# Attention and gated MLP on one core: paired items in one PSUM bank, output transposed in place, whole-tile key reads, and engine orders rewritten by a table

## The chip, the cores and the metric

The kernel runs on one core of one Trainium2 chip. A core has five engines that run side by side, each through its own list of instructions and in order: TensorE (PE) multiplies matrices and writes PSUM, VectorE (DVE) and ScalarE (ACT) read PSUM and compute elementwise, GpSimd (POOL) computes elementwise in SBUF, and SyncE (SP) issues DMA transfers. PEld is the weight-load half of PE, and SPq in a trace is SP's queue of DMA issues. PSUM has eight banks of 512 fp32 columns by 128 partitions. The metric is the device time in microseconds, lower is better.

## The reference

```
mod = silu(c) @ w_mod                       # six vectors of 640: sa, ca, ga, sb, cb, gb
h = layernorm(x) * (1 + ca) + sa            # x: 2048 tokens x 640
q, k, v = h @ wqkv                          # 32 heads of 20
o = softmax(q k^T / sqrt(20)) v             # every token against all 2048
x = x + ga * (o @ wo)
h = layernorm(x) * (1 + cb) + sb
x = x + gb * (((h @ w_gate) * (h @ w_up)) @ w_down)     # inner width 1536
```

All inputs are bf16. There are 32 x 2048 x 2048 exponentials, some 134 million, and they are the largest elementwise job by far.

## The kernel before

**Tiling.** Queries are cut into seven chunks (512 tokens, then six of 256) and heads into eight sets of four. A pair of chunk and set is an *item*. The four heads of a set lie in four strips of 32 partitions, so a score matmul has 32 rows of contraction (20 used) and four strips can work at once. The smallest job is a *unit*: one strip, 512 columns of scores for 128-row key tiles, one PSUM bank.

**Two ways to an exponential.** Most units go in twos to ACT: line 1524 writes two banks (0 and 1, or 3 and 4, by turns), line 1561 takes the exponential of 1024 columns into a slot of `PP`. The rest go to DVE in quads of four units: line 1585 reads a bank into `DB` as a scaled int16, lines 1617 and 1625 mask it into two bf16 factors in `DSS`, and their product is formed by POOL in four pieces (line 1637) or by DVE in one (line 1622). `QUADS` says how many quads each item gives to DVE. Line 2192 multiplies `PP` and `DSS` with the values `Vf` (a column of ones in front gives the softmax sum) and accumulates the item in one bank; column tiles of 32 work four abreast.

**End of an item.** `item_end_tasks` (line 1707): a DVE transpose `OT` (1717), a reciprocal of the sums (1723), the normalised `OTn` (1725, on POOL or DVE), a transpose back into `OcT` (1734), and 20-row DMA moves into `Ocp` (1746), since heads of 20 rows have to be packed into the 128-row blocks that w_o expects.

**Projections.** Queries, keys and values are multiplied while the first chunk is already in attention. Keys and queries that can't be written in place go as packed rows to `k_rows` and `q_rows` in DRAM (1276) and come back in strips of 32: `KT` by four transfers for a tile (1289), `QT` by one (1298). `Ocp` also serves as the source of zeros for `q_rows` (1450).

**MLP.** `suffix` (line 1773) does the output projection of a finished chunk, the second layernorm, gate and up, and down, in between the scores of the next chunk. Weights of gate and up stream through staging tiles (1931). For 256 tokens a gate round and an up round share one bank: DVE casts the gate half (1959), and multiplies it with the up half (1966).

**Order.** Nothing is written in order by hand. Each piece of work is a `Task` with an engine, an assumed duration and dependences; `Sched` plays them out in assumed time, and `emit_program` writes each engine's list in the order found, with semaphore waits for what comes from other engines. For PE, `pick_pe` chooses at each step: the next score if its banks are free, a DVE score that is due, attention times values, then projection and MLP work by priority. `STAGE` changes its thresholds item by item. When recent PE work falls under `FILL_MIN`, `zero_fill` adds matmuls of zeros into an open accumulator (2523). Banks 5, 6, 2 and 7 form the pool `G`, handed to whoever asks first: DVE's scores, accumulators of items, projections and MLP rounds:

```
G = Slots([5, 6, 2, 7], "G")
...
def avail(self, only=None):
    best = None
    for k, (i, rel) in enumerate(self.free):
        ...
        for r in rel:
            t = max(t, r.done + SEM)
        if best is None or t < best[0]:
            best = (t, k)
```

## Time and profile before

| | |
|---|---|
| runs shown | 804.77 us median of 3 (804.38 to 808.84) |
| span of the profiled execution | 803.8 us, first to last instruction |
| instructions in it | 37761 |
| exponentials on ACT (line 1561) | 810, 748.5 us busy |
| scores read by DVE (line 1585) | 428, 285.5 us busy |
| DMA | 64.66 MB, mean 80 GB/s |

The profiled execution is one of the same program; its own time is the span and what lies around it, and only the span has rows. "Idle before" is the time an engine stood still ahead of a group of instructions, with what ended it. Matmuls overlap, and their ends are modelled, so the busy share of PE isn't a measure of its load. Windows give busy time of each engine in a stretch, and PEclk the granted clock of PE as a share of full speed.

### The profile page before, as it was taken

Reading aid. Unit: us, or ns where it says so; the run is one execution under the profiler, and the core shown is the slowest. Engines: PE = TensorE matmul, PEld = TensorE weight load, DVE = VectorE, ACT = ScalarE, POOL = GpSimd, SP = SyncE. Lnnn points to the kernel's source line nnn. Section 1 sums busy time; section 2 is a strip of 40 time slices with the busy share of each in tenths; the row PEclk is TensorE's granted clock in tenths of the full one; section 3 lists DMA queues with packets and bytes.
Section 4 is the critical chain, followed back from the end, with each engine's and each line's share of the span. In section 5 each row is a group of like instructions: output and inputs, shape, how many; then the busy total and the mean of one; then the engine's idle time right before and its main releaser. Section 6 shows DMA issues by size and latency. Waiting matters only on the chain.

```text
span 803.8 us, 37761 instructions
## 1 busy us (share of the span) xinstructions
PE 790.4 (98%) x16595; PEld 380.6 (47%) x16595; DVE 697.8 (87%) x1401; ACT 764.8 (95%) x847; POOL 386.0 (48%) x396
## 2 busy tenths in 40 slices
PE   8999999999999999999999999999999999999998
PEld 4433433333244434445555455555555555555567
DVE  7978788799989999988999999999899988898754
ACT  6899899999999999999999999999999999999961
POOL 3347455654366565763444443545534554455300
PEclk9999999999999999999999999999999999999999
DMA  9733212212341532120032404231540254414420
GB/s 297 243 113 91 62 43 64 61 33 76 92 109 50 167 88 52 35 55 13 24 81 65 95 16 112 57 73 39 121 89 15 54 118 94 98 37 106 92 68 18
DMA packets 154314, 64.66 MB, mean 80 GB/s; under 512 B 116951, under 2 KB 154151, under 8 KB 154151
## 3 DMA queue, kind: packets, MB, share of 16 engines
q1 hardware_dynamic: 153223, 61.10, 30.0%
q8 instruction: 132, 2.16, 1.1%
q10 hardware_dynamic: 928, 1.15, 0.5%
q14 instruction: 31, 0.25, 0.1%
HBM read 50.63 MB, written 8.99 MB: 74 GB/s over the span
## 4 chain that ended last, share of the span: by engine, by line
PE 77%; ACT 14%; DVE 5%; issue 2%; DMA 1%; SPq 1%; POOL 0%; DVEq 0%; ACTq 0%
PE ps_all L1524 26%; PE ps_all L970 21%; PE ps_all L2192 19%; ACT PP L1561 14%; PE ps_all L1230 4%; PE ps_all L966 3%; DVE DB L1585 2%; PE ps_all L1889 1%; PE ps_all L1166 1%; PE ps_all L1127 1%; DVE DSS L1617 1%; PE ps_all L2523 0%; DVE DSS L1625 0%; DMA QT<-q_rows 0%; PE ps_all L991 0%
## 5 line engine op out<-in xcount | busy, mean ns | idle before, releaser
L1561 ACT ACTIVATE PP<-ps_all 128x1024 bf16<-128x1024 f32 x810 | 748.5, 1090 | 6.7 <-PE ps_all L1524 4.8
L1637 POOL TENSOR_TENSOR DSS<-DB,DSS 128x512 bf16<-128x512 bf16 x268 | 305.0, 1157 | 290.6 <-DVE DSS L1625 254.2
L1585 DVE TENSOR_SCALAR DB<-ps_all 128x512 int16<-128x512 f32 x428 | 285.5, 681 | 50.5 <-PE ps_all L1524 48.0
L1524 PE MATMUL ps_all<-QT,KT 32*128 32x256 bf16 (+2 forms) x3648 | 319.4, 287 | 4.5 <-DMA QT<-q_rows 0.8
L1524 PEld LDWEIGHTS ps_all<-QT,KT 32*128 32x128 bf16 x3648 | 93.9, 92 | 204.1 <-ACT PP L1561 141.5
L2192 PE MATMUL ps_all<-PP,Vf 128*32 128x256 bf16 (+2 forms) x2892 | 163.6, 291 | 0.5 <-DVE KPB L1242 0.3
L970 PE MATMUL ps_all<-h2T,stg 128*32 128x256 bf16 (+2 forms) x2716 | 122.9, 281 | 0.3 <-DVE DB L1585 0.2
L2192 PEld LDWEIGHTS ps_all<-PP,Vf 128*32 128x32 bf16 (+1 forms) x2892 | 54.5, 94 | 76.4 <-issue 67.6
L2192 PE MATMUL ps_all<-DSS,Vf 128*32 128x256 bf16 (+1 forms) x1512 | 88.7, 291 | 0.0
L1617 DVE TENSOR_SCALAR DSS<-DB 128x2048 int16<-128x2048 int16 x107 | 77.2, 722 | 0.8
L970 PEld LDWEIGHTS ps_all<-h2T,stg 128*32 128x32 bf16 x2716 | 61.6, 96 | 26.9 <-issue 22.0
L1625 DVE TENSOR_SCALAR DSS<-DB 128x2048 int16<-128x2048 int16 x107 | 73.2, 684 | 0.8 <-PE ps_all L2192 0.8
L970 PE MATMUL ps_all<-wd,hprod 128*32 128x320 bf16 (+1 forms) x1404 | 61.0, 277 | 0.0
L1725 POOL TENSOR_TENSOR OTn<-OT,invT 128x256 bf16<-128x256 f32 (+1 forms) x49 | 35.3, 721 | 37.7 <-DVE invT L1723 37.5
L1622 DVE TENSOR_TENSOR DSS<-DB,DSS 128x2048 bf16<-128x2048 bf16 x40 | 51.5, 1287 | 0.0
L2192 PEld LDWEIGHTS ps_all<-DSS,Vf 128*32 128x32 bf16 x1512 | 36.5, 95 | 20.9 <-issue 12.4
L970 PE MATMUL ps_all<-wV,hT 128*32 128x160 bf16 x1280 | 38.9, 236 | 0.9 <-DVE DB L1585 0.3
L970 PEld LDWEIGHTS ps_all<-wd,hprod 128*32 128x32 bf16 x1404 | 31.2, 96 | 14.2 <-issue 10.8
L1717 DVE STREAM_TRANSPOSE OT<-ps_all 128x256 f32<-128x256 f32 (+2 forms) x57 | 27.1, 475 | 8.8 <-PE ps_all L2192 8.5
L1230 PE MATMUL ps_all<-hT,wk 128*32 128x512 bf16 x360 | 32.3, 382 | 0.0
L970 PEld LDWEIGHTS ps_all<-wV,hT 128*32 128x32 bf16 x1280 | 24.6, 97 | 15.9 <-issue 8.2
L1230 PE MATMUL ps_all<-hT,wq 128*32 128x512 bf16 x375 | 31.3, 382 | 0.6 <-DVE OT L1717 0.6
(133 smaller groups left out, 556.1 us busy)
## 6 DMA issues: line engine op xcount, KB each, us to landing
stg<-in_B_w_gate_dram SPq DMA_DIRECT2D x74, 160.0 KB
stg<-in_B_w_up_dram SPq DMA_DIRECT2D x74, 160.0 KB
KT<-k_rows SPq DMA_DIRECT2D x112, 32.0 KB
QT<-q_rows SPq DMA_DIRECT2D x48, 64.0 KB
Ocp<-OcT SPq DMA_DIRECT2D x164, 10.0 KB
wm<-in_w_mod_dram SPq DMA_DIRECT2D x3, 800.0 KB
x<-in_A_x_dram SPq DMA_DIRECT2D x7, 320.0 KB
k_rows<-KPA SPq DMA_DIRECT2D x16, 128.0 KB
```

Of the source, the lines that this page charges most:

```text
L970: return lambda e, b: e.matmul(ps[32 * x:32 * x + 32, b, c0 + o:c0 + o + w], lhs()[:, 32 * x:32 * x + 32], rhs() if w == n else rhs()[:, o ...
L1230: f = [lambda e, b_, k=k, x=x: e.matmul(ps[x:x + min(32, w - x), b_, :], wx[:, k, r0 + x:r0 + min(x + 32, w)], hT[tc][:, k, :], tile_posit ...
L1524: ems.append(lambda e, i=i, kt=kt: e.matmul(dstf()[:, i * u.n:(i + 1) * u.n], KT[32 * u.s:32 * u.s + 32, u.j, kt * 128:(kt + 1) * 128], QT ...
L1561: return e.activation(PPs[g % 2][:, cellp["p"], 0:nu * 512], ps[:, b0:b0 + nu, :].rearrange("p b c -> p (b c)"), AFT.Exp, scale=ESCALE)
L1585: return e.tensor_scalar(DBl[st_["slot"]][:, x * 512:(x + 1) * 512], bank(cell["b"]), EBIAS, 0.0, op0=ALU.add, op1=ALU.max)
L1617: return e.tensor_scalar(DSl[st_["ss"][0]][:, :], DBl[st_["slot"]][:, :], 0x7F, 0x3F00, op0=ALU.bitwise_and, op1=ALU.bitwise_or)
L1622: return e.tensor_tensor(d, DBl[st_["slot"]][:, :].bitcast(BF16), d, ALU.mult)
L1625: return e.tensor_scalar(DSl[st_["ss"][1]][:, :], DBl[st_["slot"]][:, :], 0x7F80, 2, op0=ALU.bitwise_and, op1=ALU.bitwise_or)
L1637: return e.tensor_tensor(d, DBl[st_["slot"]][:, x * w:x * w + w].bitcast(BF16), d, ALU.mult)
L1717: t1 = Task("dve", n * 1.1 + 70, lambda e: e.transpose(OT[:, 0:n], ps[:, item_info[it]["bank"], 0:n].rearrange("p (b q r) -> p b r q", q=3 ...
L1725: f3 = lambda e: e.tensor_tensor(OTn[:, 0:n].rearrange("p (b c r) -> p b r c", c=32, r=2), OT[:, 0:n].rearrange("p (b r c) -> p b r c", c= ...
L2192: ems.append(lambda e, i=i, kt=kt, stt=stt, stp=stp: e.matmul(ps[32 * s:32 * s + mc, bk, 0:u.n], Vf[:, (kt * H + 4 * u.j + s) * VW:(kt * H ...
```

## The change

1. `own`, `lead`, `second`: two neighbouring items of 256 tokens share one accumulator bank, the second in columns 256 to 511. One transpose of 512, one reciprocal and two normalisations close both.
2. `OTn` is laid out so that a transpose writes `Ocp` directly; `OcT` and its DMA moves are gone. Rows of `Ocp` come in another order, so w_o is loaded in 48 pieces in that order, and its own late extra tile is gone.
3. `join_reads`: the four transfers of a key tile become one of 128 rows, at the place of the first.
4. For 256 tokens two gate rounds share a bank, and two up rounds (`GU2`): casts and products of 512 columns.
5. `Ring` and `visit`: `PP` is 16 slots of 512; a score takes the next units from a look-ahead of six, in different strips; its two output slots needn't be neighbours.
6. `QUADS`, `STAGE` and other constants change. DVE gets 109 quads in place of 107.
7. The planner's latencies get corrections by pair of engines (`seen_at`).
8. After planning, `replan` drops 14 tasks of PE, hands out the banks of `G` from a written string for what starts after 80 us of planned time, moves tasks within each engine's list by a table, and `rechain` renews the dependences on banks.

In the listing of the changed program PE has 16538 instructions (16597 before), DVE 1278 (1403), POOL 420 (400), SP 420 (709).

```
-QUADS = ((0, 4, 3, 3, 3, 4, 4, 4), (2, 2, 1, 2, 2, 2, 1, 2), (2, 2, 1, 2, 2, 2, 1, 2), (2, 2, 1, 2, 2, 2, 1, 2), (2, 2, 1, 2, 2, 2, 1, 2), (2, 2, 1, 2, 2, 2, 1, 2), (2, 1, 2, 2, 2, 1, 2, 0))
+QUADS = ((0, 5, 3, 3, 3, 4, 3, 4), (2, 2, 2, 2, 2, 2, 1, 2), (1, 2, 1, 2, 2, 2, 1, 2), (1, 3, 1, 1, 2, 2, 1, 3), (2, 2, 1, 2, 3, 1, 1, 2), (2, 2, 1, 2, 2, 1, 2, 3), (2, 1, 2, 1, 1, 2, 4, 3))
...
+PLAN_FROM = 80000.0
+PLAN = {
+    "drop": (1947, 1963, 2320, 2729, 3476, 3487, 3498, 4099, 4112, 4723, 5191, 5496, 5497, 5901),
+    "banks": (
+        "7527657577656576575677576565765672625256225562655256657627552275227752772557225722757266252652665265"
...
+    "pe": [
+        (129, 128), (153, 144), (134, 146), (135, 147), (136, 148), (137, 149), (155, 164), (166, 186), (167, 187), (168, 188),
...
+def join_reads(sc):
+    first = {}
+    for t in sc.order["sp"]:
+        if t.whole and id(t) not in first:
+            parts, f = t.whole
+            for x in parts:
+                first[id(x)] = t
+            t.emits = [f]
...
+def rebank(sc):
+    k = 0
+    for r in sc.G.recs:
+        r["move"] = r["task"] is not None and r["task"].start >= PLAN_FROM
+        if r["move"]:
+            r["i"] = int(PLAN["banks"][k])
+            r["put"](r["i"])
+            k += 1
...
+def replan(sc):
+    gone = set(PLAN.get("drop", ()))
+    sc.order["pe"] = [t for i, t in enumerate(sc.order["pe"]) if i not in gone]
+    rebank(sc)
+    for eng, moves in PLAN.items():
...
+        old = sc.order[eng]
+        gone = {a for a, _ in moves}
+        new = [t for i, t in enumerate(old) if i not in gone]
+        for a, b in moves:
+            new.insert(b, old[a])
+        sc.order[eng] = new
+    rechain(sc)
...
+                    for t in kt_ready[(j, tc)]:
+                        t.whole = (kt_ready[(j, tc)], lambda e, j=j, tc=tc: e.dma_start(
+                            KT[:, j, tc * 512:(tc + 1) * 512],
+                            bass.AP(KS.tensor, (656 * tc + 80 * j) * 512, [[DH * 512, 4], [512, 32], [1, 512]])))
...
-    d_wo = [dma("sp", 128 * KD * D * 2, lambda e: e.dma_start(wo_sb[:, :, :], wov[:, :, :]), [d_wm[3][0]], prio=10)]
+    d_wo = [[] for _ in range(KD)]
+    for j in range(NSET):
+        i0 = DH * j
+        while i0 < DH * j + DH:
+            i1 = min(DH * j + DH, i0 // 32 * 32 + 32)
+            for x in range(4):
...
+                    return e.dma_start(wo_sb[p0:p0 + i1 - i0, i0 // 32, :], A_wo[r0:r0 + i1 - i0, :])
...
+                o = PP[:, p[0]:p[-1] + 1:(p[1] - p[0] if nu > 1 else 1), :]
+                return e.activation(o, ps[:, b0:b0 + nu, :], AFT.Exp, scale=ESCALE)
...
+                OTn[:, g0:g0 + gn, DH * (j + x):DH * (j + x) + DH, :].rearrange("p b c r -> p b r c"),
...
+            def f4(e):
+                o = Ocp[slot][:, b0:b1, qo:qo + nq_].bitcast(F32).rearrange("p k (b c) -> p k b c", c=32)
+                i = OTn[:, g0:g0 + gn, 32 * b0:32 * b1, :].rearrange("p b (k c) r -> p k b (c r)", c=32).bitcast(F32)
...
+                return e.transpose(o, i)
...
+            if n <= 256 and GU2:
+                two.append((wbuf, dm))
...
+                for w_ in range(2):
+                    mms = []
+                    for x in range(2):
+                        for k in range(KD):
+                            f = qf(n, lambda k=k, cell=pair[x][0][w_]: cell["t"][:, k, :], lambda k=k: h2T[:, k, 0:n],
+                                   k == 0, k == KD - 1, x * n)
...
-            stt = first_pv[(it, s)]
+            stt = first_pv[(it, s)] and it not in lead
...
-                ps[32 * s:32 * s + mc, bk, 0:u.n],
+                ps[32 * s:32 * s + mc, binfo["bank"], c0:c0 + u.n],
...
+    join_reads(sc)
+    replan(sc)
     nw = emit_program(nc, sc)
```

1011 lines of the change are left out of this document (679 added, 332 removed), and 289 rows, old and new, of the table PLAN.

## The prediction

> **What bounds the kernel now.** I read the page's table of engines first, then its chain, and distrusted both: TensorE (PE) is busy 98% of the span and holds 77% of the chain, ScalarE (ACT) 95% and 14%. Which of the two sets the pace is not in those shares. It is in the starts of the exponentials.
>
> ```profile
> span 803.8 us, 37761 instructions
> PE 790.4 (98%) x16595; PEld 380.6 (47%) x16595; DVE 697.8 (87%) x1401; ACT 764.8 (95%) x847; POOL 386.0 (48%) x396
> PE 77%; ACT 14%; DVE 5%; issue 2%; DMA 1%; SPq 1%; POOL 0%; DVEq 0%; ACTq 0%
> ...
> L1561 ACT ACTIVATE PP<-ps_all x810: 1002/1067/1327, 16.4 to 774.7; 128x1024 bf16<-128x1024 f32 x162
> ```
>
> The last row is the view of line 1561: 810 exponentials, the first starting at 16.4 us and the last at 774.7. The same view, cut to windows, gives the next four rows (exponentials in the window, first and last start). The waits between 100 and 775 us give the fifth.
>
> ```profile
> L1561 ACT ACTIVATE PP<-ps_all x21: 1017/1130/1255, 408.6 to 426.7; 128x1024 bf16<-128x1024 f32 x21
> ...
> L1561 ACT ACTIVATE PP<-ps_all x81: 1002/1042/1230, 16.4 to 99.5; 128x1024 bf16<-128x1024 f32 x81
> ...
> L1561 ACT ACTIVATE PP<-ps_all x11: 1017/1024/1062, 87.0 to 99.5; 128x1024 bf16<-128x1024 f32 x11
> ...
> L1561 ACT ACTIVATE PP<-ps_all x138: 1017/1125/1327, 649.1 to 774.7; 128x1024 bf16<-128x1024 f32 x138
> ...
> PEld ps_all L1524 <- ACT PP L1561: 125.4, 439, 0.8
> ```
>
> Where ACT is never short of scores, 20 steps take 18.1 us: a pace of 0.905 us for each exponential. In the last row the weight load of a score waited 439 times for an exponential to free its banks, in a stage of some 730: more often than not PE is there first. So ACT's pace is the floor, and what lies above it is lateness. The span is four terms: first start 16.4; 809 steps of 0.905 = 732.1; lateness 774.7 - 16.4 - 732.1 = 26.2; and 803.8 - 774.7 = 29.1 from the last exponential's start to the end. The lateness splits: up to 99.5 us 83.1 - 80 x 0.905 = 10.7, of which 12.5 - 10 x 0.905 = 3.4 in the stretch from 87.0 on; after 99.5 us 675.2 - 729 x 0.905 = 15.5. The last 125.6 us lose only 125.6 - 137 x 0.905 = 1.6.
>
> **The change part by part.** Counts of the changed program come from its listing of instructions by engine.
>
> Exponentials: 806 in place of 810, since DVE takes 109 quads of scores instead of 107. Four steps, -3.6 us. For 464 of them the two output slots of the new ring don't lie side by side. No row shows an exponential with such an output; a gain is excluded because the element count is the same, and the nearest bound above is the step itself: at +0.01 us each, 4.6 us. I take 0, since both halves are still 512 contiguous elements.
>
> SP's queue. The timeline from 87 to 95 us shows what the stretch at 87.0 lost: four small moves of attention output stood ahead of two reads of query tiles, and a score waited for the second until 94.31. The next rows are the durations of the issues.
>
> ```profile
> 87.61 2.98 SPq L1746 DMA_DIRECT2D Ocp<-OcT  x4
> ...
> 90.71 0.92 SPq L1298 DMA_DIRECT2D QT<-q_rows  x2
> ...
> 94.31 0.40 PE L1524 MATMUL ps_all<-QT,KT 32*128 32x512 bf16 x4 [0.82 <-DMA QT<-q_rows]
> ...
> L1746 SPq DMA_DIRECT2D Ocp<-OcT x248: 549/714/1642, 59.6 to 769.2; - x124
> ...
> L1289 SPq DMA_DIRECT2D KT<-k_rows x112: 302/421/1722, 30.1 to 195.9; - x112
> ...
> L1493 SPq DMA_DIRECT2D wo<-in_A_wo_dram x4: 327/396/1384, 33.1 to 36.2; - x4
> ```
>
> All 248 output moves go (248 x 0.714 = 177 us of issue), because a transpose now writes Ocp directly. The key reads fall from 112 to 28 (84 x 0.421 = 35 us less); w_o rises from 5 issues to 48 (43 x 0.396 = 17 us more). In the new listing these two reads follow the writes of their rows at once, with nothing between, so they go out at least the 3.0 us earlier that the four moves took: of the 3.4 us lost, 3.0 come back. The key read still waits for the same writes of k_rows, but now four strips wait for 128 KB together; behind it on SP stand w_o pieces and further key reads. Its cover is the lead at which the rows are written. With the cover gone a tile would be as late as the query read above: 94.31 - 90.71 = 3.6 us, for 28 tiles at most 101 us, and earliness gains at most the three issues saved ahead of the last strip. I take 0: the view of line 1289 names no engine that waited for a key read, though the last strip's piece always went out three issues after the first. The w_o pieces are scaled before the first use at 228.8 us:
>
> ```profile
> L970 PE MATMUL ps_all<-wo,Ocp x656: 232/299/311, 228.8 to 699.7; 128*32 128x320 bf16 x116, 128*32 128x160 bf16 x48
> ```
>
> In the listing they are issued between the key reads, the last of which starts at 195.9 us in the kernel before. That is tens of microseconds of cover; without it the output projection, and the score behind it on PE, would wait.
>
> VectorE (DVE). These rows group its instructions by shape (count, busy us, mean ns).
>
> ```profile
> L1585 DVE TENSOR_SCALAR DB<-ps_all 128x512 int16<-128x512 f32 x428 | 285.5, 681 | 50.5 <-PE ps_all L1524 48.0
> L1617 DVE TENSOR_SCALAR DSS<-DB 128x2048 int16<-128x2048 int16 x107 | 77.2, 722 | 0.8
> L1625 DVE TENSOR_SCALAR DSS<-DB 128x2048 int16<-128x2048 int16 x107 | 73.2, 684 | 0.8 <-PE ps_all L2192 0.8
> L1622 DVE TENSOR_TENSOR DSS<-DB,DSS 128x2048 bf16<-128x2048 bf16 x40 | 51.5, 1287 | 0.0
> L1959 DVE CAST gsb<-ps_all 128x256 bf16<-128x256 f32 x60 | 24.6, 412 | 4.7 <-PE ps_all L970 4.6
> L1717 DVE STREAM_TRANSPOSE OT<-ps_all 128x256 f32<-128x256 f32 x47 | 20.8, 442 | 4.8 <-PE ps_all L2192 4.7
> L1966 DVE TENSOR_TENSOR hprod<-ps_all,gsb 128x256 bf16<-128x256 f32 x48 | 19.7, 413 | 0.5
> L1734 DVE STREAM_TRANSPOSE OcT<-OTn 128x128 f32<-128x128 f32 x47 | 14.2, 301 | 1.5 <-POOL OTn L1725 1.5
> L1723 DVE RECIPROCAL invT<-OT 128x8 f32<-128x8 f32 x47 | 8.9, 189 | 0.2
> L1997 DVE TENSOR_TENSOR hprod<-ps_all,gsb 128x512 bf16<-128x512 f32 x12 | 8.1, 677 | 0.4 <-PE ps_all L970 0.4
> L1986 DVE CAST gsb<-ps_all 128x512 bf16<-128x512 f32 x12 | 8.1, 674 | 0.5 <-PE ps_all L970 0.5
> L1717 DVE STREAM_TRANSPOSE OT<-ps_all 128x512 f32<-128x512 f32 x8 | 5.7, 712 | 1.4 <-PE ps_all L2192 1.3
> L1725 DVE TENSOR_TENSOR OTn<-OT,invT 128x256 bf16<-128x256 f32 x5 | 3.1, 620 | 0.0
> ```
>
> Paired items: 46 transposes of 256 go, 23 of 512 come: -20.3 + 16.4 = -3.9; 23 reciprocals fewer: -4.3; 28 transposes of 128 fewer (two of double size more, about 0.9): -7.5. Gate and up in pairs: 60 casts and 60 products of 256 become 30 and 30 of 512: -4.5 and -4.5. Two quads more: eight score reads, two of each mask: +5.4 + 2.8. Five products of 2048 fewer: -6.4. Five more normalisations on DVE, at no more than the 0.62 us of a full one: +3.1. In all about -20 us of 697.8. DVE is not the floor, so none of it counts directly; what it buys is PSUM banks that come free sooner.
>
> GpSimd (POOL): 296 pieces of the product instead of 268, 28 x 1.157 = +32 us, covered by 290 us of its own idle time; if a product came late, the matmuls on it would be issued later.
>
> ```profile
> L1637 POOL TENSOR_TENSOR DSS<-DB,DSS 128x512 bf16<-128x512 bf16 x268 | 305.0, 1157 | 290.6 <-DVE DSS L1625 254.2
> L2523 PE MATMUL ps_all<-ident,Vf 128*32 128x256 bf16 x128 | 5.9, 275 | 0.0
> ```
>
> PE: the 128 filling matmuls of 256 columns go (5.9 us busy), and four full-width ones of w_o. Attention and projections keep their columns within 2%, kind by kind. In the two listings the stretches of one kind (scores, column tiles, full width) fall from 1651 to 1574 and the runs of scores from 802 to 777: fewer turns of the array for the same work. So PE gets further ahead of ACT, and lateness after 99.5 us should fall. How far can't be counted from rows: the ends are 0 (every score in time) and the present 15.5, or more if the written order fits badly. I take the rate that the kernel before already reaches in its last stretch, 1.6 us in 125.6, over the 660 us: 8.4.
>
> The clock. Two windows of the trace, before and during a slow stretch, give the price of leaving PE unfilled (length, busy time of PE, PEld, DVE, ACT and POOL, granted clock, DMA). The third row is the view of line 1561 across it, the last that of the filling line by slices of 20 us:
>
> ```profile
> 93.40:96.80 3.40, 2.33 (x50) 1.06 (x52) 1.75 (x4) 2.72 (x4) 3.40 (x4) 1.00 0.52 119
> 96.90:100.20 3.30, 3.30 (x44) 1.07 (x40) 1.67 (x4) 2.54 (x3) 0.07 (x1) 0.50 0.02 5
> ...
> L1561 ACT ACTIVATE PP<-ps_all x7: 1017/1024/1024, 94.7 to 101.9; 128x1024 bf16<-128x1024 f32 x7
> ...
> busy tenths in 40 slices 0004000020002102010000000000000000590000
> ```
>
> PE was busy 2.33 of 3.4 us, and the next 3.3 us ran at a granted clock of 0.50; six steps across it took 7.2 us, 1.8 above pace. After 80 us fills stood in seven slices, and all of those are dropped. The Trainium skill, "TensorE: Matmul & The Clock Gate", Part 1: The HAM clock gate, lets the clock fall only after an idle window of about 3.4 us; by that rule the dropped fills cost nothing, and the sum stays. The row is harsher than the rule, since a window two thirds busy sufficed. By the row a fill costs nothing only while PE stays about as busy as the 98% of the page; I take 0 and keep seven times 1.8, 12.6, as the upper end.
>
> The start is nearly the same program up to the first exponential, 16.4. After it three more casts of hT go to ACT at the 0.77 us of the first row below. ACT waited 1.5 us ahead of a single cast in that stage (second row), so I count them as covered (2.3 us if not).
>
> ```profile
> L1133 ACT ACTIVATE hT<-ps_all,mcol 128x512 bf16<-128x512 bf16 x2 | 1.4, 774 | 2.9 <-PE ps_all L1127 2.9
> ...
> 35.26 0.59 ACT L1180 CAST KT<-ps_all 128x512 bf16<-128x512 f32 x1 [1.49 <-PE ps_all L1166]
> ```
>
> The end: the work of PE behind the last score is the same gate, up and down matmuls of the last rows; I keep 29.1, within 1 either way.
>
> **Sum.** 16.4 + 805 x 0.905 (728.5) + (10.7 - 3.0) + 8.4 + 29.1 = 790.1 us of span, against 803.8. The median of the runs shown, 804.8, lies 1.0 above the span of the profiled execution, so 791.1.
>
> **The rivals.** (a) *Lateness nearly vanishes.* The order on every engine is written out; if durations hold, scores are late only by the remnants: early 5, later 2. 16.4 + 728.5 + 7 + 29.1 + 1 = 782. For it: 439 waits of PE for ACT. Against: no long stretch of the kernel before is free of lateness.
> (b) *The clock takes the gain.* Without the fills half-clock windows open at five of the seven places: 791 + 5 x 1.8 = 800. For it: the two windows above. Against: the fills stood between stretches that are 98% busy.
> (c) *The gain stops at the counted parts.* The new order is no better than the old: 4 steps and the query read, 804.8 - 3.6 - 3.0 = 798. For it: most of the 26.2 us of lateness has no single cause in the waits. Against: PE has less to do, and fewer turns.
> (d) *Shared banks turn into the wait: slower.* Two items keep one PSUM bank, twice as long; gate and up take a bank for a 0.67 us cast or product instead of about 0.41; keys, values, DVE's scores and items share four banks whose next user is now fixed by a table. PE runs in order, so one late bank delays the next exponential's score. The table hands out some 715 banks. It decides the sign at 791 + 14 = 805, that is 20 ns of lateness for each hand-out; at 40 ns it adds 28.6: 820. For it: PE already loses time to score reads by DVE, in the rows below. Against: those are about 10 us of 675, and DVE gets 20 us lighter.
>
> ```profile
> PEld ps_all L970 <- DVE DB L1585: 5.4, 19, 0.5
> PEld ps_all L2192 <- DVE DB L1585: 4.6, 20, 0.4
> ```
>
> That the change doesn't do what it says is excluded for the transfers: the listing shows 28 key reads and no output move.
>
> **How the numbers follow.** Chances: the forecast 0.66, (a) 0.12, (b) 0.06, (c) 0.07, (d) 0.09. The likeliest gives 791. One per cent, about what a measurement of this kernel can tell from no change, is 8 us: faster means below 796.7. Forecast and (a) are faster, 0.78; (b) and (c) lie within, 0.13; (d) is slower, 0.09. The range runs from 780, just under (a), to 802, which takes in (b), (c) and an output pattern or uncovered casts that cost their upper ends; outside are (d) and a little on either side.
>
> **What would show it.** 806 exponentials whose first start is within 1 us of 16.4, with a pace of 0.905 in their best stretch; a last start near 761; no query read in PE's waits around 90 us; a granted clock of 1.00 in every later window; DVE near 678 us busy, POOL above 400. The forecast is wrong if the pace itself is longer (the split output), if idle time of weight loads names DVE or gate and up casts for tens of microseconds (d), or if the stretch behind the last exponential grows beyond 31 us.

## The result, and the profile after

The changed kernel takes 809.68 us (median of 10 runs, 808.35 to 816.02) against 804.56 us before (median of 10, 803.61 to 808.84): a ratio of 1.0071, with a 95% interval of 1.0047 to 1.0095. It is slower by some 5 us where 791 was forecast, which is outside the range of 780 to 802 and on the other side of no change, though within 1%. Two of the ten executions, 815.47 and 816.02, had a mean granted clock of 0.987, the other eight 0.994 or 0.996.

The page of the changed kernel (span, busy time by engine, chain that ended last):

```profile
span 807.2 us, 36873 instructions
...
PE 790.3 (98%) x16536; PEld 379.6 (47%) x16536; DVE 700.7 (87%) x1276; ACT 759.6 (94%) x847; POOL 411.8 (51%) x416
...
PE 65%; ACT 21%; DVE 6%; issue 4%; DMA 2%; SPq 1%; POOL 0%; ACTq 0%; DVEq 0%
```

As before, these shares tell little: PE is at 98% in both, and DVE, meant to get lighter, is at 700.7 us where it was at 697.8. Line 3090 is the exponential now. Its view over the whole span and in four windows (count, duration min/median/max, first and last start):

```profile
L3090 ACT ACTIVATE PP<-ps_all x806: 1002/1177/1342, 23.8 to 777.6; 128x1024 bf16<-128x1024 f32 x162
...
L3090 ACT ACTIVATE PP<-ps_all x73: 1002/1044/1267, 23.8 to 99.3; 128x1024 bf16<-128x1024 f32 x73
...
L3090 ACT ACTIVATE PP<-ps_all x734: 1017/1182/1342, 99.3 to 777.6; 128x1024 bf16<-128x1024 f32 x184
...
L3090 ACT ACTIVATE PP<-ps_all x32: 1017/1062/1304, 499.2 to 529.5; 128x1024 bf16<-128x1024 f32 x32
...
L3090 ACT ACTIVATE PP<-ps_all x82: 1017/1144/1329, 698.8 to 777.6; 128x1024 bf16<-128x1024 f32 x82
```

The same view of the kernel before, in the same two late stretches:

```profile
L1561 ACT ACTIVATE PP<-ps_all x34: 1017/1086/1172, 499.1 to 529.5; 128x1024 bf16<-128x1024 f32 x34
...
L1561 ACT ACTIVATE PP<-ps_all x83: 1017/1179/1327, 699.7 to 774.7; 128x1024 bf16<-128x1024 f32 x83
```

The four terms of the forecast can be read off these rows. The last column is an experiment told below, the changed kernel without the moves in SP's list.

| us | before | forecast | after | without SP's moves |
|---|---|---|---|---|
| first exponential starts | 16.4 | 16.4 | 23.8 | 16.8 |
| steps of 0.905 | 732.1 | 728.5 | 728.5 | 728.5 |
| lateness to about 99 us | 10.7 | 7.7 | 75.5 - 72 x 0.905 = 10.3 | 82.4 - 79 x 0.905 = 10.9 |
| lateness after that | 15.5 | 8.4 | 678.3 - 733 x 0.905 = 14.9 | 670.7 - 726 x 0.905 = 13.7 |
| last start to the end | 29.1 | 29.1 | 29.6 | 29.1 |
| span | 803.8 | 790.1 | 807.2 | 799.0 |

The 17.1 us between forecast and span are, up to rounding, 7.4 at the start, 2.6 of early lateness, 6.5 of later lateness, and 0.5 behind the last exponential.

**The later lateness is not spread out.** From 499.2 to 529.5 us the changed kernel loses 30.3 - 31 x 0.905 = 2.2 (before, 30.4 - 33 x 0.905 = 0.5), and from 698.8 on 78.8 - 81 x 0.905 = 5.5 (before, 75.0 - 82 x 0.905 = 0.8). That leaves 7.2 for the other 569 us, where the kernel before lost 14.2. So in the middle the new order halves the lateness, at the forecast's rate (569 x 1.6 / 125.6 = 7.2). What it wins there it gives back at both ends.

**The start.** SP's and ACT's timelines (start, duration, engine and line, what it waited for), first of the kernel before:

```profile
1.18 0.42 SPq L857 DMA_DIRECT2D x<-in_A_x_dram  x1
1.64 0.46 SPq L861 DMA_DIRECT2D wm<-in_w_mod_dram  x1
...
5.02 0.74 ACT L1034 ACTIVATE xn<-x 128x640 bf16<-128x640 bf16 x1 [0.23 <-DMA x<-in_A_x_dram]
```

and of the changed kernel, with one row of PE's:

```profile
1.17 0.42 SPq L1422 DMA_DIRECT2D wm<-in_w_mod_dram  x1
1.63 8.98 SPq L1418 DMA_DIRECT2D x<-in_A_x_dram  x2
...
9.33 0.74 ACT L1595 ACTIVATE xn<-x 128x640 bf16<-128x640 bf16 x1 [4.72 <-DMA x<-in_A_x_dram]
...
12.88 0.80 PE L1552 MATMUL ps_all<-scol,wm 128*128 128x1 bf16 x25 [5.02 <-DVE scol L1574]
```

The table's first two moves on SP, (2, 1) and (4, 3), put the 800 KB of `wm` ahead of the first x tile, and the second x tile ahead of wk. The first x tile is asked for only 0.45 us later, but ACT can use it at 9.33 instead of 5.02. PE has nothing to do meanwhile: `wm` itself must wait for `scol`, which stands behind x's statistics in DVE's list. The windows of the two kernels (length, busy time of PE, PEld, DVE, ACT, POOL, granted clock, DMA share, GB/s), before:

```profile
7.90:12.80 4.90, 4.80 (x89) 3.20 (x93) 3.36 (x10) 2.08 (x4) 1.59 (x3) 1.00 1.11 339
13.10:20.00 6.90, 6.58 (x152) 3.35 (x145) 6.34 (x22) 6.69 (x11) 2.80 (x5) 1.00 1.00 309
```

and after:

```profile
7.90:12.80 4.90, 0.00 (x0) 0.00 (x0) 2.47 (x14) 2.55 (x7) 1.82 (x4) 1.00 0.41 122
13.10:20.00 6.90, 6.90 (x83) 4.40 (x83) 3.94 (x13) 3.02 (x6) 1.19 (x3) 0.51 0.97 302
```

PE stands still for 4.9 us, and the next 6.9 us run at a granted clock of 0.51.

### The profile page after: what moved, and what is told of

Read it like the earlier page. It is cut to its first block, busy times and chain, and to the rows that moved or that the text cites. A ratio compares the mean times of both kernels' runs of the same rounds, so it can differ in the third digit from the quotient of the medians.

```text
span 807.2 us, 36873 instructions
## 1 busy us (share of the span) xinstructions
PE 790.3 (98%) x16536; PEld 379.6 (47%) x16536; DVE 700.7 (87%) x1276; ACT 759.6 (94%) x847; POOL 411.8 (51%) x416
## 4 chain that ended last, share of the span: by engine, by line
PE 65%; ACT 21%; DVE 6%; issue 4%; DMA 2%; SPq 1%; POOL 0%; ACTq 0%; DVEq 0%
PE ps_all L2121 23%; ACT PP L3090 21%; PE ps_all L1531 19%; PE ps_all L2801 15%; PE ps_all L1791 3%; PE ps_all L1527 2%; DVE DB L2148 1%; DMA x<-in_A_x_dram 1%; DVE DSS L2184 1%; DVE st L1632 1%; DMA stx<-in_B_w_gate_dram 1%; DVE DSS L2192 1%; DMA stg<-in_B_w_up_dram 1%; SPq L2488 1%; PE ps_all L1688 1%
## 5 line engine op out<-in xcount | busy, mean ns | idle before, releaser
L2204 POOL TENSOR_TENSOR DSS<-DB,DSS 128x512 bf16<-128x512 bf16 x296 | 345.1, 1192 | 276.8 <-DVE DSS L2192 233.3
L2801 PE MATMUL ps_all<-PP,Vf 128*32 128x256 bf16 (+3 forms) x2876 | 158.0, 288 | 0.0
L1531 PE MATMUL ps_all<-h2T,stg 128*32 128x256 bf16 (+2 forms) x2808 | 113.0, 278 | 0.0
L2801 PE MATMUL ps_all<-DSS,Vf 128*32 128x256 bf16 (+3 forms) x1544 | 95.0, 289 | 0.5 <-POOL DSS L2204 0.5
L2801 PEld LDWEIGHTS ps_all<-PP,Vf 128*32 128x32 bf16 (+1 forms) x2876 | 67.7, 95 | 46.1 <-issue 39.4
L2184 DVE TENSOR_SCALAR DSS<-DB 128x2048 int16<-128x2048 int16 x109 | 85.8, 787 | 3.8 <-PE ps_all L2801 1.7
L2192 DVE TENSOR_SCALAR DSS<-DB 128x2048 int16<-128x2048 int16 x109 | 78.2, 717 | 1.9 <-PE ps_all L2801 1.7
L2801 PEld LDWEIGHTS ps_all<-DSS,Vf 128*32 128x32 bf16 (+1 forms) x1544 | 40.1, 96 | 19.5 <-issue 15.1
L2286 POOL TENSOR_TENSOR OTn<-OT,invT 128x160 bf16<-128x160 f32 (+1 forms) x44 | 24.1, 568 | 30.9 <-DVE invT L2281 30.8
L1791 PE MATMUL ps_all<-hT,wk 128*32 128x512 bf16 (+1 forms) x360 | 31.0, 384 | 0.0
L2275 DVE STREAM_TRANSPOSE OT<-ps_all 128x512 f32<-128x512 f32 (+2 forms) x34 | 23.1, 678 | 7.5 <-PE ps_all L2801 7.2
```

What stands on the lines that cost most here:

```text
L1531: return lambda e, b: e.matmul(ps[32 * x:32 * x + 32, b, c0 + o:c0 + o + w], lhs()[:, 32 * x:32 * x + 32], rhs() if w == n else rhs()[:, o ...
L1791: f = [lambda e, b_, k=k, x=x: e.matmul(ps[x:x + min(32, w - x), b_, :], wx[:, k, r0 + x:r0 + min(x + 32, w)], hT[tc][:, k, :], tile_posit ...
L2184: return e.tensor_scalar(DSl[st_["ss"][0]][:, :], DBl[st_["slot"]][:, :], 0x7F, 0x3F00, op0=ALU.bitwise_and, op1=ALU.bitwise_or)
L2192: return e.tensor_scalar(DSl[st_["ss"][1]][:, :], DBl[st_["slot"]][:, :], 0x7F80, 2, op0=ALU.bitwise_and, op1=ALU.bitwise_or)
L2204: return e.tensor_tensor(d, DBl[st_["slot"]][:, x * w:x * w + w].bitcast(BF16), d, ALU.mult)
L2275: t1 = Task("dve", n * 1.1 + 70, lambda e: e.transpose(OT[:, 0:n], ps[:, item_info[it]["bank"], 0:n].rearrange("p (b q r) -> p b r q", q=3 ...
```

## The experiments

My theory after this reading: SP's list has two faults, the late x and, from 700 us on, late weight reads; the rest of the change is worth what the forecast said. The rivals: the whole table is at fault, or the new program without any table (shared banks, wider gate and up), or only one of the two faults exists. The kernel before, run beside each experiment, had medians from 803.99 to 805.08; so a difference of 1 us or less between two experiments says little.

**The late x, from both sides.** The changed kernel without the first two moves:

```
-        (2, 1), (4, 3), (14, 12), (11, 14), (25, 17), (24, 18), (16, 20), (80, 21), (37, 22), (61, 26), (27, 28), (38, 32), (48,
+        (14, 12), (11, 14), (25, 17), (24, 18), (16, 20), (80, 21), (37, 22), (61, 26), (27, 28), (38, 32), (48,
```

> The changed kernel without the first two moves of its SP table: the first tile of x is asked for ahead of the modulation weights again, and wk ahead of the next tile of x; all else as in the changed kernel. Theory (start): the first exponential of the changed kernel starts at 23.8 us instead of 16.4 because the first 320 KB of x wait behind 800 KB of weights in one queue, and nothing later makes that good; so the first exponential goes back to 16.4 +- 0.5 and the time falls by 7.5 us, from 809.7 to about 802 (800 to 804). Rival (absorbed): the later stages are held by something else, such as TensorE's own work, and the gain is given back by the last score: first exponential 16.4, time 807 to 810. Rival (other cause): the late start comes from the other reorderings on the first 20 us and the first exponential stays above 20 us.

The kernel before with that order of its first five transfers:

```
+    first5 = sc.order["sp"][:5]
+    moved = [first5[i] for i in (0, 2, 1, 4, 3)]
...
+    sc.order["sp"][:5] = moved
```

> The kernel before with nothing changed but the order of its first five transfers on SP: c, modulation weights, x, x, wk in place of c, x, weights, wk, x. Theory (start): this alone moves the first exponential from 16.4 to about 23.8 us and the time from 804.6 to about 812 (810 to 814), with a stretch of half clock between 13 and 20 us. Rival (absorbed): the delay is made good behind the start, 805 to 808. Rival (other cause): no change within 1 us.

The changed kernel with 21 more matmuls on PE in the gap, so that x is as late but the clock stays up:

```
+    t = sc.order["pe"][17]
+    t.emits = t.emits * 22
```

> The changed kernel with x still behind the modulation weights, and 21 more filling matmuls (4.5 us at 0.216 us) on TensorE in the 5 us in which it stands idle before the modulation sums (7.9 to 12.9 us). Theory (two prices): x lands 4.3 us later, and the rest of the 7.0 us is the half clock from 13 to 20 us that the idle stretch brings; with TensorE kept busy the clock stays at 1.00, the first exponential starts near 21 us instead of 23.8 and the time falls by 2.5 to 3 us, from 809.7 to about 807. Rival (x alone): the first exponential stays within 0.5 us of 23.8. Other rival (fills in the way): later than 24.

The first gave 804.68 us, ratio to before 0.9999 (0.9981 to 1.0017), with the first exponential at 16.9. The second made the kernel before slower, 810.17, ratio 1.0079 (1.0052 to 1.0106), with the first exponential at 22.2, 5.8 later. The third gave 807.92, ratio 1.0033 (1.001 to 1.0055). Its windows:

```profile
7.90:12.80 4.90, 4.90 (x24) 2.07 (x22) 2.43 (x14) 2.55 (x7) 1.79 (x4) 1.00 0.43 123
13.10:20.00 6.90, 6.89 (x132) 4.26 (x132) 5.53 (x18) 4.31 (x9) 1.97 (x4) 1.00 1.01 318
```

and its view of the exponentials:

```profile
L3096 ACT ACTIVATE PP<-ps_all x806: 1000/1177/1342, 21.1 to 776.2; 128x1024 bf16<-128x1024 f32 x162
```

The clock stays at 1.00, and the first exponential starts at 21.1. So of the 23.8 - 16.9 = 6.9 us that the two moves cost at the start, 23.8 - 21.1 = 2.7 are the half clock, and 21.1 - 16.9 = 4.2 the late x itself. At the end of the kernel the filled gap gave 809.68 - 807.92 = 1.8, and undoing the moves gave back 5.0, not 6.9 and not the 7.5 that I expected.

**Where the rest went, and the weight reads.** The exponentials from 700 to 750 us, first of the changed kernel and then of that first experiment:

```profile
L3090 ACT ACTIVATE PP<-ps_all x54: 1017/1130/1329, 698.8 to 749.2; 128x1024 bf16<-128x1024 f32 x54
...
L3090 ACT ACTIVATE PP<-ps_all x51: 1018/1112/1315, 699.5 to 749.2; 128x1024 bf16<-128x1024 f32 x51
```

The lateness there rises from 50.4 - 53 x 0.905 = 2.4 to 49.7 - 50 x 0.905 = 4.4: with x first, 2.0 us are lost again near the end. The timeline of the same experiment, of SP and with one row of PE's:

```profile
681.76 0.53 SPq L2488 DMA_DIRECT2D stg<-in_B_w_gate_dram  x1
716.73 0.36 SPq L2667 DMA_DIRECT2D out_dram<-xck  x1
717.13 0.44 SPq L2488 DMA_DIRECT2D stg<-in_B_w_up_dram  x1
...
734.42 0.29 PE L1531 MATMUL ps_all<-h2Tt,stg 128*32 128x256 bf16 x4 [1.74 <-DMA stg<-in_B_w_up_dram]
```

and SP's waits there (idle us, times, longest):

```profile
SPq L2667 <- DVE xck L2658: 34.4, 1, 34.4
```

An output write stands in SP's list ahead of the weights of the last rows, and waits 34.4 us for DVE. Weights whose staging tiles are free wait behind it; then they go out in a burst, and an up weight is 1.74 us late for PE; from 736 to 740 us the granted clock is 0.68. The changed kernel has the same wait, up to 723.35, and the same late read, 1.10 us, with the clock at 1.00. The cure that follows is to read four weights ahead of that write:

```
+    up = [lst[i] for i in (378, 391, 388, 403)]
...
+    sc.order["sp"] = lst[:377] + up + [t for t in lst[377:] if t not in up]
```

> The run with x first, and four reads of gate and up weights that stood behind two output writes on SP put ahead of them: their buffers were free by 680 us in that run, but SP waited 34.4 us (682.3 to 716.7) for the residual sum that the output write needs, and 13 reads then left in one burst. Theory (queue): the wait of 1.7 us of a gate/up weight load for its read near 732 us and the late steps up to 738 us go, 4.4 - 0.7 = 3.7 us of lateness in that run's stretch from 700 to 750; the profiled span falls from 802.5 to about 799 and the median from 804.7 to 800 to 802, with less scatter. Rival: the burst is held by the DMA rate, not by the queue's order, and another read is late instead: no change within 1 us.

It gave 801.56, ratio 0.9968 (0.9945 to 0.9991): 3.1 faster than with the first two moves undone alone. The wait of PE for weights is gone, and lateness from 700 to 750 us falls from 4.4 to 1.4. But five of its twelve executions took 802.8 to 807.2, and the profiled one of these, 804.92, has another late read:

```profile
138.53 0.38 PE L2130 MATMUL ps_all<-QT,KT 32*128 32x512 bf16 x1 [2.54 <-DMA KT<-k_rows]
```

A score waits 2.54 us for a key read, and the granted clock is 0.58 over the next 3.3 us.

**All of SP's moves, and the whole table.** The changed kernel with none of the 254 moves on SP, everything else kept:

```
-    "sp": [
-        (2, 1), (4, 3), (14, 12), (11, 14), (25, 17), (24, 18), (16, 20), (80, 21), (37, 22), (61, 26), (27, 28), (38, 32), (48,
...
+    "sp": [],
```

> The changed kernel with the table's moves for SP left out, all 254 of them; its moves for the other engines, its banks and its dropped fills stay. Theory (SP's order is what failed): the late first tile of x, the late weights near 739 us and the late scores of the last 15 us all come from SP's new order; first exponential at 16.9, lateness after 100 us about the 8.4 of the prediction, 791 to 797. Rival (two faults only): SP's order costs the 7.0 us at the start and the 3.7 us of the late read, the rest of the lateness lies in the order of TensorE: 799 to 802, like the run with four reads moved. Rival (the SP moves belong to the others' order): without them reads come later than the other engines' order needs, 805 or more.

and with no table at all:

```
-    replan(sc)
```

> The changed kernel without the step that rewrites the orders and the banks by the table: its planner's own order on every engine, its own bank choices, all filling matmuls kept; key tiles read by one transfer each, paired items and late w_o pieces remain. Theory: first exponential at 16.4 (x is first on SP here); lateness between 100 and 700 us is larger than the 10.6 us of the changed kernel, near the 15 us of the kernel before, since the table is what took it down; so about 804 (800 to 809). Rival: the lateness came down through paired items and wider gate and up tiles, not the table: 798 to 800.

Without SP's moves it takes **801.09 us** (800.38 to 802.28), ratio to before 0.9944 (0.9926 to 0.9962): faster than both kernels, but not the 791 to 797 that I expected if SP's order were the whole fault. Its view of the exponentials:

```profile
L3064 ACT ACTIVATE PP<-ps_all x806: 1002/1183/1342, 16.8 to 769.9; 128x1024 bf16<-128x1024 f32 x162
...
L3064 ACT ACTIVATE PP<-ps_all x80: 1002/1042/1241, 16.8 to 99.2; 128x1024 bf16<-128x1024 f32 x80
...
L3064 ACT ACTIVATE PP<-ps_all x727: 1018/1193/1342, 99.2 to 769.9; 128x1024 bf16<-128x1024 f32 x182
...
L3064 ACT ACTIVATE PP<-ps_all x74: 1018/1190/1312, 699.5 to 769.9; 128x1024 bf16<-128x1024 f32 x74
```

Without any table it takes 806.09, ratio 1.0017 (1.0004 to 1.003). So SP's part of the table costs 809.68 - 801.09 = 8.6 us, the rest of the table gains 806.09 - 801.09 = 5.0, and the whole costs 3.6. By the median it ends where mending the two faults ended, at 801, so the other moves on SP together are worth nothing in a typical execution. A third fault that strikes only some executions isn't excluded: all eleven without SP's moves lie below 802.3, while five of twelve with the two faults mended lie above, and the one of these that has rows shows the late key read. And 801 is still 10 above the forecast.

**Key reads.** Four transfers for a key tile again, once in the kernel without the table, and once in the one without SP's moves:

```
-    join_reads(sc)
```

> As the run without the table, and the key tiles read back in four transfers of one strip each again, 112 reads instead of 28. Theory (the prediction's zero for this part): the time is within 1 us of the run without the table, and no engine waits for a key read in either. Rival: one transfer for a whole tile makes the tile usable later, so four transfers are faster by 1 us or more. Other rival: 84 more issues on SP delay other reads, slower by 1 us or more.

> The run without SP moves, with the key tiles read back in four transfers of one strip each, 112 instead of 28. The prediction's zero: within 1 us of the 801.1 of that run. Theory (with w_o in 48 pieces on the same queue between the key reads, 84 more issues make key tiles late, as in the run without the table, where a score waited 1.7 us for a key read at 60.8 us and a half clock followed): 803 to 808, with more scatter.

The first took 810.25, ratio 1.0069 (1.0049 to 1.0089), 4.2 above the same kernel with joined reads; the second 805.38, ratio 1.0004 (0.9982 to 1.0025), 4.3 above. Ten of the second's twelve executions have a mean granted clock below 1.0, and none of the eleven with joined reads. Rows of the second (its profiled execution took 807.90), first of PE's and SP's timelines:

```profile
60.64 0.61 PE L2095 MATMUL ps_all<-QT,KT 32*128 32x512 bf16 x3 [2.51 <-DMA KT<-k_rows]
...
53.07 4.08 SPq L2064 DMA_DIRECT2D wo<-in_A_wo_dram  x7
57.20 1.99 SPq L1824 DMA_DIRECT2D KT<-k_rows  x4
```

then of its windows:

```profile
57.00:60.00 3.00, 1.13 (x11) 0.21 (x9) 1.86 (x4) 1.50 (x2) 0.00 (x0) 0.94 0.20 49
60.00:75.00 15.00, 14.36 (x132) 3.59 (x132) 8.55 (x13) 9.98 (x10) 5.85 (x4) 0.56 0.44 108
```

With joined reads, of SP's timeline:

```profile
53.69 0.53 SPq L1829 DMA_DIRECT2D KT<-k_rows  x1
```

and of the same windows:

```profile
57.00:60.00 3.00, 2.77 (x31) 0.76 (x29) 2.51 (x6) 2.65 (x4) 0.00 (x0) 1.00 0.53 150
60.00:75.00 15.00, 14.69 (x219) 5.33 (x216) 14.45 (x23) 14.94 (x17) 11.27 (x9) 1.00 0.43 113
```

Seven small w_o pieces stand ahead of the key read in both. With four strips for each of this and the earlier tiles SP has issued the last strip at 57.20 + 1.99 = 59.2 us; the joined read is issued by 53.69 + 0.53 = 54.2. The score is 2.51 us late, and the clock is 0.56 over the next 15 us, where it is 1.00 with joined reads.

**Shared banks, and wider gate and up.** Each undone, without the table (the orders are planned anew, with the planner's other constants left as they are, so these are not prices of the one edit alone):

```
-PAIRS = 1
+PAIRS = 0
```

> The run without the table, and items no longer paired in one PSUM bank. Theory (the prediction's: pairs lighten VectorE and shorten nothing directly): VectorE busy some 8 us longer, time within 3 us of the 806.1 without the table. Rival (shared banks are a wait): 3 us or more faster than 806.1. Other rival (pairs are what took the lateness down): 3 us or more slower.

```
-GU2 = 1
+GU2 = 0
```

> The run without the table, and gate and up tiles of 256 columns again instead of pairs of 512. Theory: VectorE busy some 9 us longer, time within 3 us of 806.1. Rival (the wide tiles hold PE and a bank too long between scores, as near 522 us, where two stretches of 40 matmuls stand around one run of scores): 3 us or more faster. Other rival (the wide tiles are what took the lateness down): 3 us or more slower.

818.33, ratio 1.0162 (1.0131 to 1.0194), and 822.52, ratio 1.0214 (1.0176 to 1.0251), against 806.09. DVE's busy time rises by 7.5 us in each (682.4 to 689.9 and 690.0). I had expected less than 3 us of difference. Undoing either makes the kernel 12 or 16 us slower, which speaks against sharing as the wait that the changed kernel lost its time to; the table's own choice of banks was not undone alone.

**The query read.** The kernel before, with the two query reads ahead of the four output moves:

```
+    read = sp[97:99]
...
+    sc.order["sp"] = sp[:93] + read + sp[93:97] + sp[99:]
```

> The kernel before, with its two query reads at 90.7 us put on SP ahead of the four moves of attention output. The prediction's step: the reads go out up to 3.0 us earlier, the wait of the score until 94.31 goes and with it the half clock behind it; 3.0 us less, about 801.7. Rival (the stage is full): TensorE has V projections and modulation sums to do between the scores of this stage, and the time falls by less than 1 us.

804.33, ratio 0.9988 (0.9967 to 1.0008). The 3.0 us that I had counted are not there. Windows of the stretch, first in the kernel before and in this run:

```profile
75.00:100.00 25.00, 23.93 (x476) 10.49 (x480) 19.00 (x42) 22.30 (x25) 14.79 (x14) 0.94 0.30 76
...
75.00:100.00 25.00, 24.69 (x523) 11.22 (x523) 20.55 (x45) 23.69 (x27) 15.03 (x15) 1.00 0.31 77
```

In the profiled executions the move does help: the clock is 1.00, ACT takes 27 exponentials where it took 25, and the span is 801.6 against 803.8. The median shows nothing of it, because the half clock behind that wait is not in a typical execution. The profiled execution of the kernel before has a mean granted clock of 0.998, which one half clock of 3.3 us makes (3.3 x 0.5 / 803.8 = 0.002). Of the 124 executions of that kernel whose clock is on record, 101 have 1.0, with a median of 804.3; the other 23 have 0.991 to 0.998 and take 805.9 to 812.5. That these 23 stall at the same place isn't shown.

Then the changed kernel and the one without SP's moves:

```profile
82.00:107.00 25.00, 24.82 (x568) 12.14 (x556) 22.28 (x44) 21.98 (x25) 14.80 (x13) 1.00 0.31 87
```

```profile
75.00:100.00 25.00, 24.83 (x566) 12.18 (x566) 22.20 (x43) 21.98 (x24) 15.29 (x14) 1.00 0.15 45
```

No query read is late in them, and the clock is 1.00, yet ACT is no busier than before: PE has 568 and 566 matmuls where it had 476, and is busy 24.8 of 25 us. Among them are value projections, of which the traces have 620 by the 80th exponential, against 568 before. So there the time went into other work of PE.

**The end.** From 699.5 us on, the kernel without SP's moves still loses 70.4 - 73 x 0.905 = 4.3 us, against 0.8 before. The last two groups of items have seven quads on DVE where they had two, and gate and up of the last rows come in fewer, later pieces (the last product at 767.7 us in the changed kernel, 755.1 before). Busy times of 25 us near the end, before and after:

```profile
750.00:775.00 25.00, 24.38 (x616) 13.53 (x608) 11.58 (x28) 25.00 (x29) 5.74 (x6) 1.00 0.48 105
```

```profile
750.00:775.00 25.00, 24.22 (x706) 14.90 (x700) 22.43 (x36) 23.99 (x27) 14.28 (x13) 1.00 0.15 37
```

DVE goes from 11.58 to 22.43 us. Is it DVE, is it PE's work, or only the order? All four of the following, and a fifth with both cuts, start from the kernel without SP's moves. The last six scores ahead, among the down matmuls:

```
+        if i % 6 == 0 and s:
+            out.append(s.pop(0))
+        out.append(t)
```

> The run without SP moves, with the last six scores put ahead among the down matmuls of the last rows on TensorE, one score after every six of them, instead of in pairs behind blocks of up to 56 matmuls. The prediction's sum (lateness and the stretch behind the last exponential are separate terms): the last exponential starts 1.5 to 2.5 us earlier and the time falls by as much, to about 799. Rival (TensorE's work sets the end): TensorE is busy 14.5 of the 15 us from 754 to 769, so what is taken from lateness comes back behind the last exponential, and the time stays within 1 us of 801.

172 matmuls of gate and up left out:

```
+    names = ("g5.7", "u5.7", "g5.9", "u5.9", "g5.11", "u5.11")
...
+        gone = set(at[2:-2])
+        lst = [t for i, t in enumerate(lst) if i not in gone]
```

> The run without SP moves, and 172 matmuls of the gate and up tiles of the last rows left out on TensorE (the middle ones of six rounds, all issued after 730 us; the last rows come out wrong by this, everything else is computed as before). At 8.0 us for 224 such matmuls they are 6.1 us of busy time. Theory (work left over for the end): with 30 exponentials to go TensorE has some 180 matmuls more to do than the kernel before had, and its work, not the scores, sets the end; without these the late scores of the last stretch go, and the time falls by 4 to 6 us, from 801.1 to 795 to 797. Rival (the chain of the last rows sets the end: last values, normalisation, gate and up, down): it falls by less than 1.5 us.

Masks and products of the last seven quads over 256 columns in place of 2048:

```
+        mw = 256 if qi >= 102 else 2048
```

> The run without SP moves, with the masks and products of the last seven quads cut to 256 of their 2048 columns on VectorE, and to 64 of 512 in each piece on GpSimd (the last rows come out wrong by this; all instructions, orders and waits stay). VectorE was busy 22.4 of 25 us from 750 to 775 in the changed kernel (11.6 before), its last product of gate and up came at 767.7 us (755.1 before), and the chain from 762 to 774.6 is all VectorE and GpSimd. Theory (VectorE is the wait of the last stage): with 0.85 + 0.85 + 0.64 + 0.69 us of masks and 3.6 us of product cut on that chain, the time falls by 2 to 4 us, from 801.1 to 797 to 799. Rival (the written order of TensorE: the down matmuls stand there and take their time whenever their input comes): less than 1 us.

120 of the last 200 down matmuls left out:

```
+    names = ("dn5.0", "dn5.1")
...
+        gone = {i for i in at[4:-4] if id(lst[i]) not in need}
```

> The run without SP moves, with 120 of the 200 down matmuls of the last full rows left out (the last rows come out wrong by this). They start at 761 us and later, and at 7.8 us for 200 are 4.7 us of TensorE. Theory (VectorE is the wait of the last stage): 0 to 2 us faster, since TensorE then waits for what VectorE and GpSimd still have to make. Rival (TensorE's written order from 757 us on sets the end): 3.5 to 4.7 us faster, 796.4 to 797.6.

Both of these cuts:

> The run without SP moves, with both cuts at once: masks and products of the last seven quads on 256 of 2048 columns, and 120 of the 200 last down matmuls left out (the last rows come out wrong by this). Each alone took less than 1 us. Theory (two chains of nearly the same length end together, TensorE's written order and the chain through VectorE and GpSimd): with both shortened the time falls by 2.5 to 4.5 us, from 801 to about 797.5. Rival (a third thing sets the end, such as the pace of the exponentials before 757 us and the fixed 30 us behind the last one): again less than 1 us.

| | us | ratio to before | last exponential starts |
|---|---|---|---|
| no SP moves | 801.09 | 0.9944 (0.9926 to 0.9962) | 769.9 |
| last scores ahead | 802.17 | 0.9958 (0.9941 to 0.9976) | 767.8 |
| 172 gate and up matmuls less | 800.35 | 0.9950 (0.9937 to 0.9964) | 770.3 |
| short last quads | 800.98 | 0.9959 (0.9947 to 0.9972) | 769.1 |
| 120 down matmuls less | 801.02 | 0.9963 (0.9948 to 0.9978) | 769.2 |
| both cuts | 799.07 | 0.9937 (0.9923 to 0.9950) | 767.9 |

```profile
L3080 ACT ACTIVATE PP<-ps_all x806: 1002/1182/1342, 16.7 to 767.8; 128x1024 bf16<-128x1024 f32 x162
```

In the first (the row above is its exponentials) the last exponential starts 2.1 us earlier and the kernel ends no earlier: what lateness loses, the stretch behind it gains (799.4 - 767.8 = 31.6 in its profile, against 29.1). Leaving out gate and up work was my theory of work left over, and it fell: their amount is not what the end waits for. Neither cut alone is worth 1 us; together they are worth 2.0 by the medians, less than the 2.5 to 4.5 that I expected. By the ratios, 0.9937 against 0.9944 for all the work, it is less than 1 us and within the intervals; against either cut alone (0.9959 and 0.9963) both together are faster by some 2 us. So DVE's and POOL's chain of quads and PE's down matmuls run beside each other at nearly the same length, and what one cut gives the other chain hides; how much both hold up the full kernel is known only as 2 us at most. From 699.5 us to the end this kernel takes 4.3 - 0.9 = 3.4 more than forecast (70.4 x 1.6 / 125.6 = 0.9); the two cuts account for 2.0 of it at most, and 1.4 or more stays open. An order that keeps all the work and shortens both chains was not tried.

## Why the prediction was wrong, point by point

- **The start: wrong, 7.4 of the 17.1 us.** The step that failed reads "the start is nearly the same program up to the first exponential, 16.4". The first two moves on SP exchange x and `wm`, and the forecast had no term for that. The first exponential came at 23.8; the runs put 6.9 on the two moves, 4.2 for the transfer and 2.7 for the clock.
- **The query read, -3.0: wrong, 2.6.** The read is no longer late, as forecast, but the early lateness fell by 0.4 only. The same move in the kernel before gained nothing in the median. I took the wait from one execution, which had a half clock that 101 of 124 don't have, and made it a price without asking what else that stage had to do. The forecast also added 1.0 from that span to the time; where both are on record for one execution they lie 1.7 or more apart, so 791.1 was some 0.8 too low by this alone.
- **Lateness after 99 us, 8.4: half right, 6.5.** The rate was right over 569 us. It was wrong in two stretches. From 698.8 us on (5.5) late weights behind a waiting output write explain some 1 us of it (2.4 from 700 to 750 us, and 1.4 where that wait is cured); for the rest the runs show two chains of nearly equal length where DVE has more quads (2.0 at most), and leave 1.4 or more open. The 2.2 us from 499 on are not SP's order: without SP's moves they are 2.2 too, and without the table 3.6. More than half of it is one step of 2.20 us at 526.3, while PE does 40 gate and up matmuls in a row; no run changed that alone.
- **The pace, 0.905 for 806 steps: right**, also for outputs in two separate slots. In the best stretch of the changed kernel 20 steps take 18.1 us:

```profile
L3090 ACT ACTIVATE PP<-ps_all x21: 1042/1167/1292, 743.8 to 761.9; 128x1024 bf16<-128x1024 f32 x21
```

  Its trace has 464 exponentials with two separate slots, as counted; the median step behind them is 0.904, as behind the others.
- **Key reads, taken as 0: wrong, but inside the bounds given.** Joining them is worth 4.3 us beside the w_o pieces. It isn't in the 17.1, because the kernel before had no such pieces to stand behind: the change made this wait and removed it again.
- **DVE at 678, and "none of it counts": wrong twice.** These rows are the masks of the changed kernel and POOL's products:

```profile
L2204 POOL TENSOR_TENSOR DSS<-DB,DSS 128x512 bf16<-128x512 bf16 x296 | 345.1, 1192 | 276.8 <-DVE DSS L2192 233.3
...
L2184 DVE TENSOR_SCALAR DSS<-DB 128x2048 int16<-128x2048 int16 x109 | 85.8, 787 | 3.8 <-PE ps_all L2801 1.7
L2192 DVE TENSOR_SCALAR DSS<-DB 128x2048 int16<-128x2048 int16 x109 | 78.2, 717 | 1.9 <-PE ps_all L2801 1.7
```

  The counts fell as forecast, but a mask takes 787 and 717 ns where it took 722 and 684. Without the table they take 705 and 686 and DVE is at 682.4; there a product of POOL overlaps 12 of the first masks, in the changed kernel 30. So it is the table's order that puts masks beside products. And in the last stage, where DVE is busy 22.4 of 25 us, its quads count, though only together with PE's down matmuls.
- **The tail, 29.1: right as a number (29.6), wrong as a term.** Near the end it isn't independent of lateness, as the run with the last scores ahead shows (31.6); without the table it is 804.3 - 771.2 = 33.1.
- **POOL above 400 (411.8), no price for the dropped fills: right.** The clock is 1.00 in every window of the profiled execution after 80 us. Rival (b) falls for the typical execution; where the two at 0.987 lost their clock no row shows.
- **Rival (d), the one for slower, falls by its mechanism.** Idle time of weight loads from 80 to 780 us in the changed kernel, by who ended it (us, times, longest):

```profile
PEld ps_all L2121 <- ACT PP L3090: 140.0, 496, 0.6
...
PEld ps_all L2121 <- DVE DB L2148: 9.7, 32, 0.5
...
PEld ps_all L1531 <- DVE DB L2148: 6.8, 31, 0.4
```

  About 16 us wait for score reads by DVE, not tens more than the 10 of before; 496 waits are for ACT. The kernel is slower, but not for that reason, and the prediction had no rival for SP's own order: only the query and key reads were priced by what they stand behind, the first transfers and the weights not at all.

## What to carry to other kernels

Where a table or a planner reorders DMA issues, price each exchange by what the moved transfer now stands behind, its bytes and its waits, and not by the issue; the first transfers of a kernel come first, since nothing covers them. A write that waits for a late result holds up every read behind it on its queue, and reads whose buffers are free belong ahead of it. Before a wait that goes is counted as a gain, check that a typical execution has it at all, and read how busy the engines are in that stage alone: with PE at 24.8 of 25 us the time can be filled with other work.

## What the runs showed of the hardware

- **A transfer behind a large one.** 320 KB asked for 0.45 us later, behind 800 KB instead of ahead of it, could be used 9.33 - 5.02 = 4.31 us later. The Trainium skill, "DMA: Bandwidth & Descriptors", Queues, rings and completion order, says that SP has one ring on each SDMA engine, and that each SDMA engine takes descriptors in ring order; by that rule the tile has to wait for most of the 800 KB, and the trace agrees.
- **The clock falls with PE partly busy.** After 4.9 us without PE work it was 0.51 for 6.9 us. The Trainium skill, "TensorE: Matmul & The Clock Gate", Part 1: The HAM clock gate, names an idle window of about 3.4 us as the cause of a low clock, and this row agrees. But with four-transfer key reads a window in which PE was busy 1.13 of 3.0 us (idle for 2.51 us at a stretch) was followed by 0.56 over 15 us, which the rule doesn't cover; the measurement decides.
- **Masks beside products.** Of the 109 first masks in the changed kernel, the 79 that no product of POOL overlapped took 691 ns on average, and the other 30 some 1042, taken from the single instructions' starts and durations. In the kernel before it is 87 at 684 and 20 at 884.
